# One addition and one reciprocal per head, in place of one of each for a pair of heads, in a fused attention and mixture-of-experts kernel

## The chip, the cores and the metric

The kernel runs on one core of a Trainium2 chip. The metric is the device time of one execution in microseconds (us). The core has five engines that matter here: TensorE (PE, matrix products; its weight loads are shown as PEld), VectorE (DVE), ScalarE (ACT), GpSimd (POOL), and SyncE (SP, which issues most of the DMAs). Each engine works through its own list of instructions in order; an instruction that needs the result of another engine waits for a semaphore, and everything behind it on its engine waits too.

## The reference, cut to what matters

Three layers follow one another: attention with a forget gate (4 batches, 8 heads, 576 positions, head size 64), a feed-forward layer (512 to 2048 to 512), and a mixture of experts where each token goes to its best one of 8 experts. The change touches the softmax of the attention alone:

```
scores = scale * q @ k.T + decay, with -1e9 above the diagonal
scores = scores - max(scores, axis=-1)
attn = exp(scores)
attn = attn / (sum(attn, axis=-1) + 1e-09)
out = attn @ v
```

## The kernel before, in words

The attention works on pairs of heads: 16 pairs `i` (four batches of four pairs). Each pair is cut into five units `c`, taken in the order 4, 3, 2, 1, 0. Units 0 to 3 are 128 rows of queries for each of the two heads, with 128 x (c + 1) columns of keys; unit 4 takes the last 64 rows of both heads in one tile of 128 x 576 and counts as one "head" (called `None`). So a pair has four units of two heads and one unit of one.

For each unit, `unit` (line 532 and around) lets PE compute the scores into one of two buffers in PSUM (tiles `SR`, `SRx`). Then `head` runs once for each head, as a chain of steps:

- DVE adds the decay and the mask, writes the scores into a tile `P`, and reduces each row's extreme into column `n` of a small tile `st` (128 x 8; line 582);
- ACT takes the exponential in place and adds up each row into column `2 + n` of `st` (line 587; the trace shows it as an ACTIVATE and a short read of the accumulator);
- DVE adds 1e-9 to the sums (line 592) and takes the reciprocal (line 594);
- POOL multiplies `P` by the reciprocal (line 598);
- PE transposes `P` in blocks of 128 (line 612), and DVE (head 0 of the two widest units, line 630) or ACT (the others, line 632) copies the result out of PSUM.

In the kernel before, lines 592 and 594 are issued once per unit, by head 0, for the columns of both heads together, after both heads' exponentials (event `summed`); head 1 waits for event `scaled`. Unit 4 has one column.

When all units of a pair are transposed, `weighted` multiplies by the values (lines 652 and 705) and stores the pair's output `xT` as tile `xs` to memory. A pair of heads needs eight of the `P` tiles at most (there are eight, so four units of two heads can be under way), and there are two PSUM buffers for transposes.

The order of all instructions is fixed while the program is built, by a small planner. Every step is a coroutine that asks for an engine with a planned duration and a priority (`Use("DVE", 150, fn, 0)`): the planner simulates the engines, always issues the waiting request of the lowest priority number, and adds a latency before the next step (130 ns after DVE, 150 ns after ACT, 135 ns after POOL, 200 ns after PE). Priorities: 0 for the addition, the reciprocal, the multiplication on POOL, the transposes and their copies; 0.8 for the scores and for the conversion of weights; 1 for lines 582 and 587; 1.5 for the transposes of q and k (line 442); 6 to 7 for the feed-forward layers. Planned times shape the order alone; on the chip each instruction starts when its engine is free and its semaphores are there.

Beside the attention run two other things. First, the weights of the first half of the feed-forward layer are converted in 16 pieces (tiles `wax`, `wa`): ACT (line 823), four operations on DVE (824 to 830), ACT (834), POOL (835). One piece at a time goes through, since there is one buffer `wx`. Second, the feed-forward layer's first half (tiles `hp`, `accp`, lines 880 and 1009; its elementwise steps are lines 892 to 902) takes blocks of 256 tokens. Block 0 (`px0`) is built straight from the first four pairs; a block needs all 16 pieces of weights, and there is one buffer for a block's input until the attention is over. Until the first batch is done, PE is filled with products whose result is thrown away (`warm`, line 729), at the lowest priority.

Of the kernel before, what the change touches and what calls it, by code (L numbers as in the profile page):

```python
# [14 lines left out]
ALU = mybir.AluOpType  # L15
# [60 lines left out]
class Order:  # L76
# [90 lines left out]
    def done(self, ev):  # L167
        ev.n -= 1
        if ev.n == 0:
            for g in ev.waiters:  # L170
                self.at(self.now, lambda g=g: self.step(g, None))
            ev.waiters = []

    def give(self, res, ids):
        res.ids += ids
        while res.waiters:
            gen, n = res.waiters[0]
            got = res.take(n)
            if got is None:
                return  # L180
            res.waiters.pop(0)
            self.at(self.now, lambda gen=gen, got=got: self.step(gen, got))
# [8 lines left out]
def dve(n, fn, prio=5.0, fast=False):  # L191
    return Use("DVE", 144 + n * (0.6 if fast else 1.05), fn, prio)


def act(n, fn, prio=5.0, more=0.0):
    return Use("ACT", 155 + n / 1.2 + more, fn, prio)


def pool1(n, fn, prio=5.0):
    return Use("POOL", 400 + 0.7 * n, fn, prio)  # L200
# [16 lines left out]
def mm(n, k=1):  # L217
    return k * max(111.0, n * 0.458)
# [5 lines left out]
def kernel(  # L224
# [14 lines left out]
    nc = tc.nc  # L239
# [22 lines left out]
    go, give, done = o.spawn, o.give, o.done  # L262
# [250 lines left out]
    def unit(i, c, started):  # L513

        yield qk_ok[i]
        heads = (None,) if c == 4 else (0, 1)
        gp_ = yield (p_b, len(heads))
        sl = yield (sr_b, ((0, 1), (2, 3)))
        bank = SR[sl[0] // 2]
        done(started)  # L520
        (qt, kt), z, _ = qkt[i]
        w = P * (c + 1) if c < 4 else S

        def scores():
            if c == 4:
                for n in range(2):
                    nc.tensor.matmul(bank[:, n, :S // 2], z, kt[:, S // 2 * n:S // 2 * (n + 1)],
                                     start=True, stop=i >= NSUM)
                return
            for j in range(2):  # L530
                p = slice(64 * j, 64 * j + 64)
                nc.tensor.matmul(bank[:, j, :w], qt[p, P * c:P * c + P], kt[p, :w],  # L532
                                 start=True, stop=i >= NSUM)

        def sums():
            n3 = 3 * NH
            if i == 0:
                for n in range(2):
                    if c == 4:
                        nc.tensor.matmul(bank[:, n, :S // 2], pick,  # L540
                                         cum[:NH, S // 2 * n:S // 2 * (n + 1)], start=False, stop=True)
                    else:
                        p = slice(64 * n, 64 * n + NH)
                        nc.tensor.matmul(bank[:, n, :w], ident[p, 65 * n:65 * n + 1].to_broadcast(
                            [NH, P]), cum[p, :w], start=False, stop=True)
                return
            if c == 4:
                for n in range(2):
                    nc.tensor.matmul(bank[:, n, :S // 2], picks[:n3, P * i:P * i + P],
                                     parts[:n3, S // 2 * n:S // 2 * (n + 1)], start=False, stop=True)  # L550
                return
            for j in range(2):
                h = 64 * (2 * i + j)
                nc.tensor.matmul(bank[:, j, :w], picks[:n3, h:h + 1].to_broadcast([n3, P]),
                                 parts[:n3, :w], start=False, stop=True)
        yield Use("PE", max(440, 1.72 * w), scores, 0.8, full=0.8)
        done(s_done[i])
        if i < NSUM:
            yield parts_there if i else sums_there
            yield Use("PE", mm(w if c < 4 else S // 2, 2) if i else 1.72 * w, sums, 0.8)  # L560
        yield cm_ok[i, c]
        st = ap.tile([P, 8], F32, tag="st", name=f"st{i}_{c}", bufs=10)
        summed, scaled = Event(len(heads)), Event()
        left = Event(len(heads))
        for n, j in enumerate(heads):
            p = ap.tile([P, S], F32, tag="P", name=f"P{i}_{j}{c}", bufs=NP_)
            go(head(i, j, c, p, [gp_[n]], bank, st, summed, scaled, left))
        yield left
        give(sr_b, sl)

    def head(i, j, c, p, gp_, bank, st, summed, scaled, left):
        w = P * (c + 1) if c < 4 else S
        n = j or 0
        k = 2 if c < 4 else 1
        pw = p[:, :w]
        cm, c4, _ = cms[i]
        if c < 4:
            so, pv_ = bank[:, j, :w], pw
            m = cm[:, j, :w] if i >= NSUM else cm[:, 0, 512 - w:]
        else:  # L580
            so, m, pv_ = bank[:, :, :S // 2], c4, p.rearrange("p (a b) -> p a b", a=2)
        yield dve(w + 80, lambda: nc.vector.tensor_tensor_reduce(  # L582
            out=pv_, in0=so, in1=m, scale=-0.125, scalar=3e38,
            op0=ALU.add, op1=ALU.min, accum_out=st[:, n:n + 1]), 1)
        done(left)
        done(read_ok[i, c])
        yield act(w, lambda: nc.scalar.activation(pw, pw, AF.Exp, bias=st[:, n:n + 1], scale=-1.0,  # L587
                                                  accum_out=st[:, 2 + n:3 + n]), 1, 330)
        done(summed)
        if n == 0:  # L590
            yield summed
            yield Use("DVE", 150, lambda: nc.vector.tensor_scalar(
                st[:, 4:4 + k], st[:, 2:2 + k], 1e-9, None, ALU.add), 0)
            yield Use("DVE", 150, lambda: nc.vector.reciprocal(st[:, 6:6 + k], st[:, 4:4 + k]), 0)  # L594
            done(scaled)
        else:
            yield scaled
        yield pool1(w, lambda: nc.gpsimd.tensor_scalar(pw, pw, st[:, 6 + n:7 + n], 1.0, ALU.mult,  # L598
                                                       ALU.mult), 0)
        yield pt_ok[i, j]  # L600
        dst = pt4[i][0] if c == 4 else pt[i, j][0]
        for part in ((0, 1, 2, 3), (4,)) if c == 4 else (tuple(range(c + 1)),):
            gt = yield (t_b, 1)
            T = psa.tile([P, 512], F32, tag=f"T{gt[0]}", name=f"T{i}_{j}{c}{part[0]}", bufs=1)
            last = part == (4,)

            def turn():
                for n, kb in enumerate(part):
                    if last:
                        nc.tensor.transpose(T[:64, :P], p[:, 512:S], ident)  # L610
                    else:
                        nc.tensor.transpose(T[:, P * n:P * n + P], p[:, P * kb:P * kb + P], ident)  # L612
            yield Use("PE", mm(P, len(part)), turn, 0)
            if last or c < 4:
                give(p_b, gp_)
            if c == 4:
                n = P * len(part)
                src, dh = (T[:64, :P], dst[:64, 512:]) if last else (T, dst[:, :512])
            else:
                n = w  # L620
                src = T[:, :w].rearrange("p (k q) -> p k q", q=P)
                if c < 2:
                    dh = dst[:, P * c:P * c + 384 * (c + 1)].rearrange(
                        "p (k q) -> p k q", q=384)[:, :, :P]
                else:
                    a0 = P * (c - 2)
                    dh = dst[:, a0:a0 + 384 * (c + 1)].rearrange(
                        "p (k q) -> p k q", q=384)[:, :, 256:]
            if j == 0 and c >= 2:
                yield dve(n, lambda: nc.vector.tensor_copy(dh, src), 0)  # L630
            else:
                yield act(n, lambda: nc.scalar.copy(dh, src), 0)  # L632
            give(t_b, gt)
        done(last_ok[i] if c == 4 else heads_ok[i])
# [100 lines left out]
    def attention():  # L735
        go(forget_rows())
        go(prep())
        yield Use("POOL", 3000, setup, 0)
        go(keep_warm(xs_ok[0]))
        yield sums_there  # L740
        go(loadv(0))
        for i in range(NP):
            if i + 1 < NP:
                go(loadv(i + 1))
            if i == NPAIR:
                go(hand_over())
            go(decays(i))
            go(take_pt(i))
            go(free_qk(i))
            go(weighted(i))  # L750
            for c in SEQ:
                ev = Event()
                go(unit(i, c, ev))
                yield ev
# [888 lines left out]
```

## Time and profile before

| | |
|---|---|
| median of 3 runs | 872.46 us (870.70 to 873.15) |
| profiled execution | 871.59 us, span of its instructions 870.0 us |
| busy: PE / PEld / DVE / ACT / POOL | 842.5 / 692.7 / 463.2 / 363.6 / 301.6 us |
| mean granted TensorE clock | 0.993 of 2.4 GHz |
| attention's last addition (line 592) | starts at 303.8 us |

The busy time of PE is partly modelled, since matrix products are pipelined: a PE that is busy for a whole stretch had no gap, but need not be at its peak. Gaps are named by what ended them. The profile's times are us from the start of the span.

### The profile page before, as it was taken

What the parts mean: (1) busy time and instruction counts of PE and PEld (TensorE: products, weight loads), DVE (VectorE), ACT (ScalarE), POOL (GpSimd) and SP (SyncE); (2) the same over time, 40 slices, a digit from 0 to 9 for tenths busy, and PEclk for the clock granted to TensorE, in tenths of its full rate; (3) what the DMA queues carried; (4) which work ended last, traced back from release to release, by engine and by line L of the source; (5) the groups of instructions that cost most, each with busy time, mean ns of one, the idle gap of its engine ahead of it and who ended that gap; (6) DMA issues with size and microseconds to landing.
All of it is one profiled execution on the core that took longest, in us unless ns stands there. A gap on an engine that the chain in (4) does not pass through costs nothing. (4 is left out here: it accounts for less than half of the span.)

```text
span 870.0 us, 15066 instructions
## 1 busy us (share of the span) xinstructions
PE 842.5 (97%) x5384; PEld 692.7 (80%) x5384; DVE 463.2 (53%) x1104; ACT 363.6 (42%) x842; POOL 301.6 (35%) x405
## 2 busy tenths in 40 slices
PE   9999997999999999999899999999999999999994
PEld 6765775887787799999888888888998888886683
DVE  7797977766545537767843354377643512112120
ACT  5677666565656635444533242323333112112010
POOL 2566876555544533444342122222210033000000
PEclk9999999999999999999999999999999999999998
DMA  7997666474324154323601135744431111721210
GB/s 144 179 188 178 157 165 155 119 144 118 92 80 132 46 137 97 108 93 100 225 34 49 73 122 156 213 154 142 146 112 49 48 49 49 288 75 64 82 49 25
DMA packets 153659, 100.90 MB, mean 116 GB/s; under 512 B 102724, under 2 KB 125764, under 8 KB 153584
## 3 DMA queue, kind: packets, MB, share of 16 engines
q1 hardware_dynamic: 150608, 95.43, 40.1%
q0 software_dynamic: 2784, 4.21, 1.8%
q8 instruction: 43, 0.70, 0.4%
q10 hardware_dynamic: 192, 0.30, 0.1%
q14 instruction: 32, 0.26, 0.1%
HBM read 76.33 MB, written 23.84 MB: 115 GB/s over the span
## 5 line engine op out<-in xcount | busy, mean ns | idle before, releaser
L902 POOL TENSOR_TENSOR glr<-gr,ghr 128x512 fp32r<-128x512 f32 x36 | 46.9, 1304 | 146.9 <-PE accBr L1009 87.1
L598 POOL TENSOR_SCALAR P<-P,st 128x512 f32<-128x512 f32 (+3 forms) x128 | 76.6, 611 | 39.2 <-DVE st L594 25.6
L880 PE MATMUL hr<-rx,wb 128*128 128x512 f32 (+1 forms) x384 | 88.7, 365 | 0.0
L880 PE MATMUL hm<-mx,wm 128*128 128x512 f32 (+1 forms) x336 | 87.4, 381 | 0.0
L1009 PE MATMUL accp<-ghp,wa 128*128 128x256 f32 x576 | 83.4, 287 | 2.1 <-DVE x_7b L1038 1.7
L587 ACT ACTIVATE P<-P,st 128x512 f32<-128x512 f32 (+3 forms) x128 | 71.4, 559 | 33.5 <-DVE st L582 32.4
L911 DVE SCALAR_TENSOR_TENSOR glm<-hm,ghm 128x512 fp32r<-128x512 f32 x36 | 24.8, 689 | 103.4 <-PE accBm L1017 68.7
L1009 PEld LDWEIGHTS accp<-ghp,wa 128*128 128x128 f32 x576 | 73.6, 191 | 5.4 <-issue 2.2
L910 ACT ACTIVATE ghm<-hm 128x512 fp32r<-128x512 f32 x36 | 21.5, 598 | 132.9 <-PE accBm L1017 111.6
L880 PEld LDWEIGHTS hr<-rx,wb 128*128 128x128 f32 x384 | 65.9, 189 | 12.2
L880 PEld LDWEIGHTS hm<-mx,wm 128*128 128x128 f32 x336 | 61.0, 188 | 15.6 <-issue 3.4
L902 POOL TENSOR_TENSOR glp<-gp,ghp 128x512 fp32r<-128x512 f32 x36 | 48.7, 1353 | 60.8 <-ACT ghp L901 54.3
L582 DVE CUSTOM_DVE_ANT_0 P<-SR,cm 128x512 f32<-128x512 f32 (+3 forms) x96 | 45.2, 485 | 24.9 <-PE SR L532 21.7
L612 PE MATMUL T<-ident,P 128*128 128x128 f32 x320 | 52.4, 278 | 3.4 <-POOL P L598 2.9
L632 ACT COPY pt<-T 128x512 f32<-128x512 f32 (+2 forms) x96 | 35.2, 391 | 36.5 <-PE T L612 35.7
L892 ACT ACTIVATE tr<-hr,quarter 128x512 f32<-128x512 f32 x36 | 24.7, 687 | 61.1 <-DVE gr L897 42.4
L532 PE MATMUL SR<-kt,qt 64*128 64x384 f32 (+3 forms) x224 | 45.7, 485 | 4.2 <-DVE st L582 4.1
L1017 PE MATMUL accm<-wm,ghm 128*128 128x512 f32 x160 | 49.0, 395 | 0.0
L612 PEld LDWEIGHTS T<-ident,P 128*128 128x128 f32 x320 | 36.8, 141 | 14.5 <-POOL P L598 6.3
L896 DVE SCALAR_TENSOR_TENSOR gr<-tr 128x512 f32<-128x512 f32 x36 | 25.9, 719 | 41.4 <-POOL glr L902 39.8
L1009 PE MATMUL accr<-ghr,wb 128*128 128x512 f32 (+1 forms) x160 | 47.1, 376 | 0.0
L1009 PE MATMUL accp<-glp,wa 128*128 128x256 f32 x288 | 46.3, 283 | 0.4 <-POOL glp L902 0.4
(348 smaller groups left out, 1858.9 us busy)
## 6 DMA issues: line engine op xcount, KB each, us to landing
cm<-rows SPq DMA_DIRECT2D x24, 256.0 KB, 4.7
rawq<-in_q_dram SPq DMA_DIRECT2D x64, 72.0 KB, 3.6
rawk<-in_k_dram SPq DMA_DIRECT2D x64, 72.0 KB, 3.0
xs<-xT SPq DMA_DIRECT2D x16, 288.0 KB, 2.1
x2n<-nat SPq DMA_DIRECT2D x18, 256.0 KB, 3.1
war<-in_moe_w_in_dram SPq DMA_DIRECT2D x8, 512.0 KB, 4.6
war<-in_moe_w_out_dram SPq DMA_DIRECT2D x8, 512.0 KB, 4.2
rawv<-in_v_dram SPq DMA_DIRECT2D x32, 128.0 KB, 2.7
```

Source lines behind the costliest of these rows:

```text
L532: nc.tensor.matmul(bank[:, j, :w], qt[p, P * c:P * c + P], kt[p, :w], start=True, stop=i >= NSUM)
L582: yield dve(w + 80, lambda: nc.vector.tensor_tensor_reduce(out=pv_, in0=so, in1=m, scale=-0.125, scalar=3e38, op0=ALU.add, op1=ALU.min, ac ...
L587: yield act(w, lambda: nc.scalar.activation(pw, pw, AF.Exp, bias=st[:, n:n + 1], scale=-1.0, accum_out=st[:, 2 + n:3 + n]), 1, 330)
L598: yield pool1(w, lambda: nc.gpsimd.tensor_scalar(pw, pw, st[:, 6 + n:7 + n], 1.0, ALU.mult, ALU.mult), 0)
L612: nc.tensor.transpose(T[:, P * n:P * n + P], p[:, P * kb:P * kb + P], ident)
L632: yield act(n, lambda: nc.scalar.copy(dh, src), 0)
L880: nc.tensor.matmul(oo, a[:, c, cs], x[c], start=(ip == 0 and c == 0), stop=(ip == 2 and c == KC - 1))
L896: yield dve(n, lambda: nc.vector.scalar_tensor_tensor(g, t, 0.5, t, ALU.min, ALU.mult), 2)
L902: yield pool2(n, lambda: nc.gpsimd.tensor_tensor(gl, g, f32(gh), ALU.subtract), 1)
L911: yield dve(n, lambda: nc.vector.scalar_tensor_tensor(gl, oo, 0.0, f32(gh), ALU.max, ALU.subtract), 2)
L1009: nc.tensor.matmul(acc[d][:, :w], b[:, fc, P * d:P * d + P], g, start=(fc == 0 and ip == 0 and (not narrow or d % 2 == 0)), stop=(fc == NF ...
L1017: nc.tensor.matmul(acc[a], g[:, P * a:P * a + P], b[:, fc], start=(fc == 0 and ip == 0), stop=(fc == NF - 1 and ip == 2))
```

## The change

Each head does its own addition and its own reciprocal, on its own column of `st`, as soon as its own exponential is there. The events `summed` and `scaled` go. The planned durations are 80 and 100 ns for the one-column operations, where 150 and 150 ns stood for two. Unit 4 is issued as before, with the new planned durations. The priority stays 0.

```
-            go(head(i, j, c, p, [gp_[n]], bank, st, summed, scaled, left))
+            go(head(i, j, c, p, [gp_[n]], bank, st, left))
...
-        done(summed)
-        if n == 0:
-            yield summed
-            yield Use("DVE", 150, lambda: nc.vector.tensor_scalar(
-                st[:, 4:4 + k], st[:, 2:2 + k], 1e-9, None, ALU.add), 0)
-            yield Use("DVE", 150, lambda: nc.vector.reciprocal(st[:, 6:6 + k], st[:, 4:4 + k]), 0)
-            done(scaled)
-        else:
-            yield scaled
+        yield Use("DVE", 80, lambda: nc.vector.tensor_scalar(
+            st[:, 4 + n:5 + n], st[:, 2 + n:3 + n], 1e-9, None, ALU.add), 0)
+        yield Use("DVE", 100, lambda: nc.vector.reciprocal(st[:, 6 + n:7 + n], st[:, 4 + n:5 + n]), 0)
```

## Rows read from the trace of the kernel before

**Rows 1.** The page, section 1: busy us, share of the span, instructions.
```profile
PE 842.5 (97%) x5384; PEld 692.7 (80%) x5384; DVE 463.2 (53%) x1104; ACT 363.6 (42%) x842; POOL 301.6 (35%) x405
```
**Rows 2.** Stretches: from:to, length, busy PE, PEld, DVE, ACT, POOL (instructions), clock, DMA share, GB/s.
```profile
15.00:86.00 71.00, 67.29 (x489) 45.49 (x489) 58.35 (x184) 51.17 (x140) 42.74 (x65) 0.98 0.89 175
86.00:150.00 64.00, 58.15 (x469) 45.17 (x468) 52.53 (x145) 42.76 (x112) 47.77 (x69) 1.00 0.67 159
150.00:310.00 160.00, 159.88 (x1282) 127.09 (x1282) 92.23 (x301) 96.14 (x261) 83.92 (x150) 1.00 0.42 103
...
130.00:140.00 10.00, 5.55 (x33) 3.77 (x33) 8.74 (x22) 6.37 (x18) 7.42 (x12) 1.00 0.80 157
```
**Rows 3.** The same view for the filler tile `warm` alone: PE and PEld busy.
```profile
15.00:86.00 71.00, 18.18 (x114) 15.62 (x114) 0.98 0.89 175
```
**Rows 4.** Waits of PE from 15 to 150 us: total us, times, longest.
```profile
PE SR L532 <- DVE st L582: 4.1, 4, 2.7
PE T L612 <- POOL P L598: 2.9, 6, 0.8
```
**Rows 5.** Timeline: start, us, engine, line, operation; the 15th weight piece and its user.
```profile
132.54 1.28 POOL L835 TENSOR_TENSOR wa<-wax,wa 128x512 fp32r<-128x512 f32 x1 [0.47 <-ACT wa L834]
...
134.76 0.64 PE L880 MATMUL hp<-px0h,wa 128*128 128x256 f32 x4
```
**Rows 6.** Groups of DVE instructions, whole span: count, busy us, mean ns, idle before.
```profile
L592 DVE TENSOR_SCALAR st<-st 128x2 f32<-128x2 f32 x64 | 19.4, 303 | 13.0 <-ACT P L587 13.0
...
L594 DVE RECIPROCAL st<-st 128x2 f32<-128x2 f32 x64 | 10.1, 157 | 0.7
...
L594 DVE RECIPROCAL st<-st 128x1 f32<-128x1 f32 x16 | 2.6, 160 | 0.2
```
**Rows 7.** The same groups from 15 to 150 us.
```profile
L592 DVE TENSOR_SCALAR st<-st 128x2 f32<-128x2 f32 x30 | 10.0, 334 | 4.2 <-ACT P L587 4.2
...
L594 DVE RECIPROCAL st<-st 128x2 f32<-128x2 f32 x30 | 4.6, 154 | 0.2
...
L592 DVE TENSOR_SCALAR st<-st 128x1 f32<-128x1 f32 x8 | 1.2, 146 | 1.9 <-ACT P_None L587 1.9
```
**Rows 8.** Timeline of one two-head unit at 141 us, from DVE, ACT and POOL.
```profile
141.22 0.15 DVE L592 TENSOR_SCALAR st<-st 128x1 f32<-128x1 f32 x1
141.29 0.68 DVE L582 CUSTOM_DVE_ANT_0 P<-SR,cm 128x512 f32<-128x512 f32 x1
141.34 0.72 ACT L587 ACTIVATE P<-P,st 128x512 f32<-128x512 f32 x1 [0.91 <-DVE st L582]
...
142.06 0.70 ACT L587 ACTIVATE P<-P,st 128x512 f32<-128x512 f32 x1
...
142.90 0.32 DVE L592 TENSOR_SCALAR st<-st 128x2 f32<-128x2 f32 x1 [0.84 <-ACT P L587]
...
143.60 0.69 POOL L598 TENSOR_SCALAR P<-P,st 128x512 f32<-128x512 f32 x1 [0.42 <-DVE st L594]
```
**Rows 9.** Timeline: additions of two columns and of one beside a POOL operation.
```profile
90.96 1.28 POOL L835 TENSOR_TENSOR wa<-wax,wa 128x512 fp32r<-128x512 f32 x1
91.07 1.19 DVE L592 TENSOR_SCALAR st<-st 128x2 f32<-128x2 f32 x1
...
100.58 1.27 POOL L835 TENSOR_TENSOR wa<-wax,wa 128x512 fp32r<-128x512 f32 x1 [1.56 <-ACT wa L834]
100.72 0.14 DVE L592 TENSOR_SCALAR st<-st 128x1 f32<-128x1 f32 x1
```
**Rows 10.** Timeline at the hole near 135 us: POOL, DVE, PE.
```profile
133.78 1.97 POOL L598 TENSOR_SCALAR P<-P,st 128x256 f32<-128x256 f32 x4
...
137.75 0.76 DVE L582 CUSTOM_DVE_ANT_0 P_None<-SR,cl 128x576 f32<-128x576 f32 x1 [0.74 <-POOL cl L482]
...
138.57 1.13 PE L532 MATMUL SR<-kt,qt 64*128 64x512 f32 x4 [2.73 <-DVE st L582]
```
**Rows 11.** Waits of DVE from 15 to 150 us: total us, times, longest.
```profile
DVE st L592 <- ACT P L587: 4.2, 5, 1.4
```

More of the change, by code (lines that the diff above doesn't have):

```diff
@@ L562, in unit @@
         st = ap.tile([P, 8], F32, tag="st", name=f"st{i}_{c}", bufs=10)
-        summed, scaled = Event(len(heads)), Event()
         left = Event(len(heads))
@@ L566, in unit, with head @@
             p = ap.tile([P, S], F32, tag="P", name=f"P{i}_{j}{c}", bufs=NP_)
-            go(head(i, j, c, p, [gp_[n]], bank, st, summed, scaled, left))
+            go(head(i, j, c, p, [gp_[n]], bank, st, left))
         yield left
         give(sr_b, sl)
-    def head(i, j, c, p, gp_, bank, st, summed, scaled, left):
+    def head(i, j, c, p, gp_, bank, st, left):
         w = P * (c + 1) if c < 4 else S
         n = j or 0
-        k = 2 if c < 4 else 1
         pw = p[:, :w]
```

## The prediction

> **What bounds the kernel now.** I read the page's first section, then busy time by stretches, then the waits inside the stretches that are not full. PE is busy for 842.5 of 870.0 us [rows 1], so the time is PE's work plus what PE wastes, and the change takes no work from PE. What it can alter is the waste: gaps, and filler products whose result nobody reads.
>
> The stretches say where waste can lie [rows 2]. From 150 to 310 us, the larger part of the attention, PE is busy for 159.88 of 160 us: feed-forward blocks fill whatever the attention leaves, so 34 of the 64 two-head units run under full cover. From 15 to 86 us PE is busy for 67.29 of 71 us, but 18.18 of these are filler [rows 3]: here the attention's own chain sets the pace, and DVE, busy for 58.35 us (82%), is its fullest engine. From 86 to 150 us PE idles for 64 - 58.15 = 5.85 us, 4.45 of them between 130 and 140. There the conversion of weights gates block 0: its 15th piece leaves POOL at 132.54 + 1.28 = 133.82 us, and the block's last products follow at 134.76 [rows 5]. The next block can only be loaded then. So the stretch that counts ends at about 150 us: it holds 30 units of two heads, and PE waits there for line 582 of DVE (4.1 us) and for POOL's multiplication (2.9 us) [rows 4].
>
> **The change part by part.** *Two adds for one.* In the stretch that counts, 30 two-column additions of 334 ns, 10.0 us, become 60 of one column. Eight of these stand in the same stretch at 146 ns [rows 7], so 60 x 0.146 = 8.8 us: 1.2 less. The two-column mean is high because some of these wait inside the instruction: one that starts at 91.07 us, under a POOL operation of 1.28 us, takes 1.19 us and both end within 0.02 us of each other; a one-column addition that starts at 100.72, 0.14 us into such a POOL operation, takes 0.14 us [rows 9]. So I expect the one-column form not to wait for POOL.
>
> The Trainium skill, "SBUF — State Buffer", section "Who interferes with whom", lists `tensor_scalar` among the operations that can take the port pair shared with GpSimd, the second to start being blocked for the whole instruction, and names no exception for a single column. If one column were blocked as two are, the additions would cost 60 x 0.334 = 20.0 us, 10.0 more, and the time would be about 882. The rows side with the rule for two columns and against it for one, so I give this outcome 0.02.
>
> *Two reciprocals for one.* 30 of 154 ns, 4.6 us [rows 7], become 60 at 160 ns, the one-column mean [rows 6], 9.6 us: 5.0 more. Added up, DVE's busy time in the stretch grows by 5.0 - 1.2 = 3.8 us; over all 64 units the additions go from 19.4 to 128 x 0.146 = 18.7 and the reciprocals from 10.1 to 20.5 us [rows 6], 9.7 more. But busy time overlaps: the addition at 141.22 takes 0.15 us and the next DVE instruction starts 0.07 us after it did [rows 8], so 0.08 us of it lie beside the next. With 60 more instructions, 60 x 0.08 = 4.8 us can vanish, and the net is between 3.8 - 4.8 = -1.0 and +3.8 us. I take 0: the lower end is the nearest measured overlap for every added instruction, and I keep 1 us back for those that meet a wait. After 150 us, any extra is hidden by the feed-forward products on PE.
>
> *The wait on the other head's exponential goes.* In the unit at 141 us the two exponentials start 0.72 us apart; the two-column addition starts at 142.90, after the second, and POOL's first multiplication at 143.60 [rows 8]. With its own addition head 0 can go 0.7 us sooner (0.4 for the narrowest unit, by the difference of lengths), and POOL then multiplies for head 0 while ACT is at head 1, so the unit's last multiplication is earlier as well, by about one multiplication or 0.5 to 0.7 us. What is late next is DVE itself, at 82%, so the pace of units hardly changes; the gain shows where a pair ends. The first batch's end, which lets block 0 start, comes about 0.5 us sooner: -0.5.
>
> That head 0 really need not wait for head 1 shows in the same rows: head 0's exponential writes its column of `st` from 141.34 while head 1's reduction on DVE, 141.29 to 141.97, still writes another. Columns of the tile are tracked apart.
>
> *The hole near 135 us.* There four multiplications stand in a row on POOL, 1.97 us, the mask of the next pair's tile comes behind them, DVE waits for that mask, and PE waits 2.73 us for DVE [rows 10]. Spread over two shorter stints, POOL would let the mask in earlier; I take -0.5 of the 4.45 us, an estimate between 0 and all of it, since the order is laid out anew.
>
> *The planner.* Planned DVE time per unit goes from 300 to 360 ns, and the steps that follow are planned sooner for head 0. Every instruction behind the first unit may so change its place, on all engines. That has no row; its bounds are what is wasted in the stretch that counts: downwards the 5.85 us of gaps, upwards what the rivals below give.
>
> Sum on the profiled execution: 871.6 + 0 - 0.5 - 0.5 = 870.6 us (span 870.0 and 1.6 around it, less 1.0). That execution lies 0.87 below the median of 872.46, so the forecast is 871.5.
>
> **The rivals.**
>
> *Faster: the hole closes.* If the new order lets the mask past the multiplications, the 4.45 us between 130 and 140 go, and the time is 872.5 - 4.5 = 868.0. For it: the one wait of 2.73 us and the chain behind it [rows 10], which passes through the very multiplications that move. Against it: block 0's last products sit behind the 15th weight piece at 133.82 us [rows 5], which the change does not touch.
>
> *Slower: DVE stands in line for head 0.* Each addition waits on DVE for ACT, and DVE takes nothing behind it meanwhile: the next head's line 582, the copies of transposes, the weight conversion, and through them PE's scores and ACT's exponentials. Now 5 of 30 do so in the stretch that counts, 4.2 us [rows 11]. With 60 additions in the place of 30, and the first of each two issued before the second exponential is done, another 4.2 us come on an engine that has little to spare: 872.5 + 4.2 = 876.7. It decides once DVE's idle time before line 592 exceeds about 7 us in the stretch. Against it: 25 of 30 never waited, because the planner reckons the exponential longer (912 ns for 512 columns, by its formula) than the 0.72 us that it takes.
>
> *Slower: every instruction costs its full length.* If the overlap of 0.08 us is not to be had, the 3.8 us stand: 872.5 + 3.8 = 876.3. The Trainium skill, "VectorE: DVE Perf Modes", section "Rules for kernel authors", says of chained operations that their number is to be kept small, as the flush of the pipeline comes with each; by that the change is a loss. The row at 141.22 [rows 8] speaks against the full length.
>
> *The change does not do what it says.* If the addition for head 0 still waited for both exponentials through the shared tile, nothing would come sooner, and the time stays at about 872.5. The overlap at 141.34 [rows 8] speaks against it.
>
> **How the numbers follow.** A measurement of this kernel tells no change from a change of less than about 0.3%, 2.6 us, so "same" is 869.8 to 875.1. The forecast has 0.45. The closed hole has 0.30: the sign of the head start is for it. Standing in line has 0.14, full length 0.06, one column blocked 0.02, no effect 0.03. So faster 0.30, same 0.45 + 0.03 = 0.48, slower 0.14 + 0.06 + 0.02 = 0.22. The range reaches down past the closed hole to the whole of the gaps, 872.5 - 5.85 = 866.6, and up to the line of waits, 876.7: 866.5 to 877, with about one in ten left out at either end. The forecast's own range is 870 to 874.
>
> **What would show it.** Right: 128 one-column additions near 0.15 us with none over 0.3; reciprocals 128 at 0.16; DVE's busy time up by 8 to 11 us; POOL's first multiplication of a unit starting before the second exponential has ended; block 0's first products before 88 us; PE full from 150 to 310 us. Wrong: additions of a microsecond (blocked); PE's gaps from 86 to 150 us well above or below 5.85 us (then the order decided, one way or the other); or DVE's wait before line 592 doubled. The forecast fails altogether if PE has gaps after 150 us that the kernel before does not have.

## The result, and the profile after

The changed kernel took 878.55 us (median of 6 runs, 876.87 to 879.88), the kernel before 872.37 us beside it: a ratio of 1.0075, with a 95% interval of 1.0061 to 1.0089. It is slower, by about 6 us; I had forecast no change (871.5), and the time lies above my range of 866.5 to 877. The profiled execution took 879.88 us with a span of 878.0, 8.0 us more than the span of the kernel before, so its rows show the loss somewhat larger than the medians do.

The page of the changed kernel, section 1, answers [rows 1]. PE does the same products (20 fewer of them filler) and is counted busy for 4 us more; DVE is busy for 463.5 us with 128 more instructions.

```profile
PE 846.7 (96%) x5364; PEld 693.3 (79%) x5364; DVE 463.5 (53%) x1232; ACT 362.8 (41%) x842; POOL 301.5 (34%) x405
```

The stretches of [rows 2] in the changed kernel (length; busy PE, PEld, DVE, ACT, POOL; granted clock; DMA share; GB/s):

```profile
15.00:86.00 71.00, 67.40 (x518) 48.21 (x517) 58.54 (x217) 50.80 (x140) 43.25 (x67) 1.00 0.86 169
86.00:150.00 64.00, 56.17 (x390) 38.69 (x387) 50.50 (x166) 41.50 (x108) 42.92 (x65) 0.95 0.67 161
150.00:310.00 160.00, 160.00 (x1285) 126.55 (x1285) 94.53 (x367) 93.17 (x252) 83.09 (x149) 1.00 0.43 105
...
130.00:140.00 10.00, 7.75 (x62) 5.28 (x62) 8.40 (x34) 6.33 (x21) 7.30 (x14) 1.00 0.76 150
```

The hole between 130 and 140 us shrank from 4.45 to 2.25 us, as a rival had it, but the stretch from 86 to 150 lost more elsewhere: PE idles for 7.83 us in place of 5.85, and its granted clock is 0.95 over the stretch, where it was 1.00. The same view in steps of 2 us shows how the clock goes with the gaps:

```profile
94.00:96.00 2.00, 0.93 (x5) 0.24 (x3) 1.97 (x7) 1.48 (x3) 1.94 (x4) 1.00 0.88 253
96.00:98.00 2.00, 0.52 (x2) 0.28 (x2) 1.45 (x3) 0.78 (x3) 1.90 (x4) 1.00 0.93 143
98.00:100.00 2.00, 1.83 (x12) 1.70 (x12) 0.84 (x2) 0.96 (x3) 1.87 (x4) 0.79 0.95 127
100.00:102.00 2.00, 1.88 (x7) 0.77 (x6) 2.00 (x3) 1.29 (x3) 1.55 (x2) 0.50 0.81 245
102.00:104.00 2.00, 2.00 (x10) 0.59 (x10) 1.93 (x6) 0.76 (x2) 1.45 (x2) 0.86 0.00 1
```

PE is busy for 1.45 of the 4 us from 94 to 98; then, with work again, it runs at the lower of its two levels (0.50, that is 1.2 of 2.4 GHz) for some us. The transposes wait for POOL there, which the waits of PE from 15 to 150 us sum up (total us, times, longest), against 2.9 us of [rows 4]:

```profile
PE T L604 <- POOL P L590: 7.3, 12, 1.3
...
PE SR L532 <- DVE st L580: 0.6, 1, 0.6
```

A second loss stands outside the stretch that I had counted. First the kernel before, then the changed one, from 320 to 450 us, where the first feed-forward half ends and the second begins:

```profile
320.00:450.00 130.00, 125.65 (x956) 120.39 (x955) 92.87 (x129) 58.18 (x97) 54.09 (x41) 1.00 0.41 123
```

```profile
320.00:450.00 130.00, 123.25 (x954) 118.35 (x951) 90.46 (x129) 58.69 (x96) 58.41 (x48) 0.99 0.46 133
```

To add the losses up I take, from stretches of 2 us, three things that PE spends on nothing: idle time, busy time x (1 - granted clock), and, from the view for the filler alone, the filler's busy time.

```
us lost               before                    changed
                idle  clock  filler       idle  clock  filler
  0 to  86      5.79   1.70   27.04       5.13   0.00   24.89
 86 to 160      5.87   0.00    0.35       7.82   3.30    0.00
160 to 320      0.12   0.00    0.00       0.00   0.00    0.00
320 to 450      4.35   0.00    0.00       6.77   1.67    0.00
sum                   45.2                      49.6
```

From 86 to 160 us 4.9 us more are lost, from 320 to 450 4.1, and 4.5 fewer up to 86: 4.4 in all, of the 8.0 by which the spans differ. The filler's column is too large, though, since a filler product overlaps the products beside it: PE without the filler is busy for 822.0 us before and 826.8 us after, out of 842.5 and 846.7, so that the filler alone took 20.4 and 19.9 us. Counted so, the losses differ by 6.3 us. The other 1.7 lie inside what is counted as busy, which is modelled; I could not place them. In these two executions, then, the time went to PE's gaps and to its clock after them, at two places. Whether the additional instructions or their new order made the gaps, the two profiles alone do not say.

### The profile page after: what moved, and what is told of

Its sections match the earlier page's. It is cut to its first block, busy times and chain, and to the rows that moved or that the text cites. A ratio compares the mean times of both kernels' runs of the same rounds, so it can differ in the third digit from the quotient of the medians.

```text
span 878.0 us, 15165 instructions
## 1 busy us (share of the span) xinstructions
PE 846.7 (96%) x5364; PEld 693.3 (79%) x5364; DVE 463.5 (53%) x1232; ACT 362.8 (41%) x842; POOL 301.5 (34%) x405
## 5 line engine op out<-in xcount | busy, mean ns | idle before, releaser
L872 PE MATMUL hr<-rx,wb 128*128 128x512 f32 (+1 forms) x384 | 90.9, 371 | 2.2 <-ACT rx L857 2.2
L590 POOL TENSOR_SCALAR P<-P,st 128x512 f32<-128x512 f32 (+3 forms) x128 | 75.3, 593 | 48.0 <-DVE st L589 19.9
L894 POOL TENSOR_TENSOR glp<-gp,ghp 128x512 fp32r<-128x512 f32 x36 | 50.7, 1409 | 46.4 <-ACT ghp L893 42.7
L604 PE MATMUL T<-ident,P 128*128 128x128 f32 x320 | 54.6, 279 | 8.5 <-POOL P L590 7.3
```

Source lines behind the costliest of these rows:

```text
L872: nc.tensor.matmul(oo, a[:, c, cs], x[c], start=(ip == 0 and c == 0), stop=(ip == 2 and c == KC - 1))
L894: yield pool2(n, lambda: nc.gpsimd.tensor_tensor(gl, g, f32(gh), ALU.subtract), 1)
```

## The experiments

Theory "order": the change costs by the new order that the planner lays out, whatever the operations. Theory "cost": 128 more DVE instructions cost the time. Ratios are to runs of the kernel before on the same chip in the same session (17 to 23 runs, median 870.5 in each of the three sessions), with 95% intervals.

**1. The operations alone.** Two one-column operations stand where one of two columns stood, in the same place; PE, ACT, POOL and SP keep their instructions in the same order, all of them.

```
-            yield Use("DVE", 150, lambda: nc.vector.tensor_scalar(
-                st[:, 4:4 + k], st[:, 2:2 + k], 1e-9, None, ALU.add), 0)
+            yield Use("DVE", 150, lambda: [nc.vector.tensor_scalar(
+                st[:, 4 + m:5 + m], st[:, 2 + m:3 + m], 1e-9, None, ALU.add) for m in range(k)], 0)
-            yield Use("DVE", 150, lambda: nc.vector.reciprocal(st[:, 6:6 + k], st[:, 4:4 + k]), 0)
+            yield Use("DVE", 150, lambda: [nc.vector.reciprocal(
+                st[:, 6 + m:7 + m], st[:, 4 + m:5 + m]) for m in range(k)], 0)
```

> Kernel before, with nothing altered but the operations themselves: in the place of each two-column addition stand two one-column additions back to back, and so for the reciprocals. The order on PE, ACT, POOL and SP is the same, instruction for instruction. Theory 'order' (the new order of the instructions costs the time): 872.4 as before, within 1.5 us, DVE busy about 463 + 8 us less what is saved on blocked additions. Theory 'cost' (128 more DVE instructions cost the time): near 878.

Measured: 868.96 us, ratio 0.9986 (0.9976 to 0.9996). The operations cost nothing; they save about 1.2 us (0.3 to 2.1 by the interval). The page's first section and the two groups on DVE (count, busy us, mean ns) of this kernel:

```profile
PE 843.5 (97%) x5384; PEld 694.2 (80%) x5384; DVE 461.6 (53%) x1232; ACT 363.2 (42%) x842; POOL 301.1 (35%) x405
```

```profile
L594 DVE RECIPROCAL st<-st 128x1 f32<-128x1 f32 x144 | 17.0, 151 | 0.2
L592 DVE TENSOR_SCALAR st<-st 128x1 f32<-128x1 f32 x144 | 16.6, 143 | 23.9 <-ACT P_None L587 13.2 <-ACT P L587 10.6
```

DVE is busy for 461.6 us, 1.6 less than before, with 128 more instructions. 144 reciprocals of 151 ns would be 21.7 us laid end to end; the busy time is 17.0, because neighbours overlap. That is still 4.3 us more than the 12.7 of the 80 reciprocals before; the additions make up for it, with 16.6 us in place of 21.8, since none of them is held up beside POOL any more. "Cost" falls.

**2. Own operations without the early start.** The changed kernel, with two lines added after the exponential, so that both heads wait for both sums:

```
+        done(summed)
+        yield summed
         yield Use("DVE", 80, lambda: nc.vector.tensor_scalar(
```

> The changed kernel, but each head goes on to its own addition and reciprocal only when the exponentials of both heads are there, so that the early start of head 0 is gone and the planner lays out the order anew. Theory 'order, by the early start': back to 871 to 874. Theory 'order, by any shuffle': anywhere in 868 to 880, with no relation to 872.4. Theory 'cost': near 878.

Measured: 875.89 us, ratio 1.0063 (1.0047 to 1.0079), not to be told from the changed kernel's 1.0075. No head starts early here, and the loss is there all the same: it does not need the early start, and taking that away does not bring the old order back.

**3. Planned times alone, 80 and 100.** The kernel before, its own two-column operations, and two numbers that only the planner reads:

```
-            yield Use("DVE", 150, lambda: nc.vector.tensor_scalar(
+            yield Use("DVE", 80, lambda: nc.vector.tensor_scalar(
...
-            yield Use("DVE", 150, lambda: nc.vector.reciprocal(st[:, 6:6 + k], st[:, 4:4 + k]), 0)
+            yield Use("DVE", 100, lambda: nc.vector.reciprocal(st[:, 6:6 + k], st[:, 4:4 + k]), 0)
```

> Kernel before with its two-column operations, only planned at 80 and 100 ns instead of 150 and 150: the operations are the same, the order differs in several hundred places. Theory 'order': moves by a few us in either sense (868 to 878). Theory 'cost': 872.4 within 1 us.

Measured: 882.80 us, ratio 1.0134 (1.0119 to 1.0148). With not one operation changed, this is slower than the changed kernel. Its stretch from 320 to 440 us shows most of it, 12.7 us of gaps where the kernel before has 4.35:

```profile
320.00:440.00 120.00, 107.30 (x857) 105.65 (x856) 88.18 (x122) 53.39 (x87) 59.30 (x42) 0.97 0.41 123
```

**4. The changed kernel planned at 150 and 150.** Its operations and waits stay as they are:

```
-        yield Use("DVE", 80, lambda: nc.vector.tensor_scalar(
+        yield Use("DVE", 150, lambda: nc.vector.tensor_scalar(
...
-        yield Use("DVE", 100, lambda: nc.vector.reciprocal(st[:, 6 + n:7 + n], st[:, 4 + n:5 + n]), 0)
+        yield Use("DVE", 150, lambda: nc.vector.reciprocal(st[:, 6 + n:7 + n], st[:, 4 + n:5 + n]), 0)
```

> The changed kernel, planned at 150 and 150 ns for each one-column operation: the same operations as the changed kernel in another order. Theory 'order': moves by a few us from 878.5 in either sense (872 to 882). Theory 'cost': 878.5 within 1 us.

Measured: 876.86 us, ratio 1.0073 (1.0060 to 1.0086), the same as the changed kernel's, which by this one number would have spoken for "cost". The profile does not: the second block's first products came at 134.2 us (changed kernel 149.1, kernel before 145.2), and the time won was lost again from 320 to 450 us, with 10.2 us of gaps. Two orders can end alike by different ways.

**5 and 6. The start of the second half.** In the changed kernel SyncE issues the loads of `rx`, the second half's input, 9 us later than before, behind a load of weights for which it waits until 420.50 us. First the kernel before, then the changed one (start, us, queue, line):

```profile
411.31 0.34 SPq L814 DMA_DIRECT2D wbr<-in_moe_w_out_dram  x1
411.70 1.86 SPq L861 DMA_DIRECT2D rx<-xs  x4
```

```profile
420.50 0.37 SPq L806 DMA_DIRECT2D wbr<-in_moe_w_in_dram  x1
420.91 1.93 SPq L853 DMA_DIRECT2D rx<-xs  x4
...
432.76 0.62 PE L872 MATMUL hr<-rx,wb 128*128 128x512 f32 x2
435.08 0.49 PE L872 MATMUL hr<-rx,wb 128*128 128x512 f32 x1 [1.69 <-ACT rx L857]
436.12 9.49 PE L872 MATMUL hr<-rx,wb 128*128 128x512 f32 x33 [0.54 <-ACT rx L857]
```

PE waits for `rx` twice and then takes 9.49 us for 33 products; at full speed 48 of them took 11.05 us, so 33 take 7.6. The granted clock of that stretch, in the changed kernel:

```profile
430.00:440.00 10.00, 7.31 (x33) 5.39 (x32) 9.09 (x16) 5.98 (x12) 1.96 (x2) 0.85 0.51 160
```

Both experiments let the planner load the first block of `rx` as soon as the buffers are free:

```
-        yield half0.first_done
         yield late_ok
+        go(half1.loads((0,)))
+        yield half0.first_done
         go(gates())
-        go(half1.loads())
+        go(half1.loads(range(1, NW)))
```

> The changed kernel; the planner may load the first input block of the second feed-forward half (tile rx) as soon as the attention's buffers are free, in place of after the first half's last products. Up to about 400 us the order is that of the changed kernel. Theory 'two places' (of the 6 us lost, 2 to 4 are lost where the second half starts, on rx and the clock that falls with it): 874.5 to 876.5, no wait of PE on rx, and PE's idle time from 320 to 450 us under 5.5 us. Theory 'front' (all is lost before 160 us): 878.5 within 1 us.

> Kernel before with the same earlier load of rx. PE did not wait for rx there, so both theories expect 870 to 872.5 on the scale of 871.5 to 872.4 for the kernel before; a gain of 2 us or more would mean that the early load helps whatever the order, and that the comparison with the changed kernel says little.

Measured with the changed kernel: 875.42 us, ratio 1.0048 (1.0032 to 1.0065); with the kernel before: 870.23 us, 0.9993 (0.9980 to 1.0006). About 2.4 us of the loss go with this cause in the changed kernel, and nothing in the kernel before. The interval still touches that of the changed kernel, so the size is rough. Idle time from 320 to 450 us came out at 5.99, above the 5.5 that I had named: PE no longer waits for `rx`, but meets other short waits.

```profile
86.00:160.00 74.00, 64.90 (x487) 47.61 (x487) 59.14 (x199) 48.19 (x128) 50.40 (x79) 1.00 0.62 152
320.00:450.00 130.00, 124.01 (x957) 119.50 (x956) 94.81 (x130) 59.36 (x97) 59.26 (x49) 1.00 0.43 131
```

These rows hold a warning: up to about 365 us the order is that of the changed kernel, with even more gaps from 86 to 160, and yet the clock stayed at 1.00. The old order shows the reverse. It stands unchanged, up to there, in experiments 1 and 6 (in this order below), and the clock fell in both:

```profile
86.00:160.00 74.00, 70.04 (x531) 54.70 (x529) 58.17 (x192) 48.64 (x129) 51.86 (x79) 0.98 0.63 152
86.00:160.00 74.00, 69.04 (x517) 54.04 (x519) 56.64 (x159) 47.22 (x126) 51.83 (x78) 0.95 0.61 145
```

So from 86 to 160 us the gaps tell the two orders apart (5.9, 4.0 and 5.0 us in three executions of the old one, 7.8 and 9.1 in two of the new one), and the clock of a single execution does not (0, 1.5 and 3.0 us lost, against 3.3 and 0). The clock is to be taken as a mean over runs: span x (1 - mean granted clock) is 7.5 us in the six runs of the changed kernel, 5.3, 6.1 and 5.4 in the 17, 22 and 23 runs of the kernel before beside the experiments, and 5.8 in the six of experiment 5. By that, the clock has 1.4 to 2.2 of the 6 us.

**7, 11 and 12. Planned times alone, 155, 140 and 160.** The kernel before; the two numbers 150 and 150 become 155 and 155 (shown), 140 and 140, 160 and 160.

```
-            yield Use("DVE", 150, lambda: nc.vector.tensor_scalar(
+            yield Use("DVE", 155, lambda: nc.vector.tensor_scalar(
...
-            yield Use("DVE", 150, lambda: nc.vector.reciprocal(st[:, 6:6 + k], st[:, 4:4 + k]), 0)
+            yield Use("DVE", 155, lambda: nc.vector.reciprocal(st[:, 6:6 + k], st[:, 4:4 + k]), 0)
```

> Kernel before, its two-column operations planned at 155 ns each in the place of 150: nothing else. Theory 'order is fragile' (any small change of a planned time shuffles hundreds of instructions, and the kernel before happens to have a good order): 2 to 12 us slower, with PE's idle time and lost clock grown in the stretches from 86 to 160 and 320 to 450 us. Theory 'the early start of head 0 is what hurts': within 1.5 us of the kernel before.

> Kernel before, its two-column operations planned at 140 ns each. Theory 'order is fragile': several us off the kernel before, most likely slower (873 to 882), since the four shuffled orders so far were 5 to 12 us slower. If shorter planned times were what hurts (80 and 100 gave 12 us): slower by about 2. If longer ones (155 gave 8): not slower.

> Kernel before, its two-column operations planned at 160 ns each. Theory 'order is fragile': several us off, 873 to 882, not the same as at 155. If there were a rule in the planned time, it would lie near or above the 8.4 us that 155 lost.

Measured: 155 gives 878.97 us, ratio 1.0085 (1.0068 to 1.0101); 140 gives 880.07, 1.0114 (1.0097 to 1.0131); 160 gives 879.85, 1.0103 (1.0079 to 1.0127). A planned time altered by 5 ns, with the same operations, costs as much as the whole change did. No rule in the planned time shows: shorter and longer ones lose alike. At 155 the loss stands from 320 to 450 us, by gaps (7.5 us, 4.35 before) and clock; from 86 to 160 us, where I had expected it too, the gaps are no larger than before (5.5 us against 5.9):

```profile
86.00:160.00 74.00, 68.52 (x533) 53.59 (x532) 56.22 (x157) 47.34 (x121) 49.23 (x73) 0.98 0.63 155
...
320.00:450.00 130.00, 122.48 (x930) 117.22 (x930) 85.59 (x122) 56.09 (x93) 56.88 (x46) 0.96 0.40 126
```

**8. Filler for longer.** In the changed kernel the first batch is done sooner, and the filler stops with it:

```
-        go(keep_warm(xs_ok[0]))
+        go(keep_warm(half0.x_ok[1]))
```

> The changed kernel; the planner may use filler products on PE until the second input block is loaded (near 150 us) and not only until the first batch is done (near 80 us). Theory 'clock' (3.3 us are lost before 160 us because PE's clock falls in its gaps): granted clock 1.00 from 86 to 160 us, and 874.5 to 877. Theory 'gaps alone': the filler stands in gaps and in nobody's way, 877.5 to 879.5. If the filler delays the attention: slower than 879.5.

Measured: 874.19 us, ratio 1.0036 (1.0023 to 1.0049), clear of the changed kernel's interval: 3.4 us won by 50 more products that nobody reads.

```profile
86.00:160.00 74.00, 70.37 (x539) 53.42 (x539) 57.83 (x191) 47.52 (x127) 50.06 (x77) 1.00 0.67 154
```

PE's idle time in this stretch fell from 7.82 to 3.63 us, but for 5.4 us PE had nothing but filler (its 50 products have 8.23 us, partly beside others), so idle time and filler together rose to 9.0, and it is not the gaps that paid. Clock lost over the whole run, as a mean of its 11 runs, is 4.4 us where the changed kernel loses 7.5 in another session: 3.0 of the 3.4 us, if the sessions may be compared (the kernel before moved between 5.3 and 6.1). The filler also moves some hundreds of instructions on all engines, from 93 us on, so a share of order in the gain is not excluded.

**9. Both mends together**, in the changed kernel: the edits of experiments 5 and 8.

```
-        go(keep_warm(xs_ok[0]))
+        go(keep_warm(half0.x_ok[1]))
...
-        yield half0.first_done
         yield late_ok
+        go(half1.loads((0,)))
+        yield half0.first_done
         go(gates())
-        go(half1.loads())
+        go(half1.loads(range(1, NW)))
```

> The changed kernel with both: the earlier load of rx and the filler until the second input block. Theory 'two places' (the front, by gaps and clock, and the start of the second half are separate losses): the gains add, 2.4 and 3.4 us off the changed kernel's 1.0075 of the kernel before, so 1.0005 to 1.002, about 871.5 to 872.5 on a scale of 870.5. If both remove the same loss: 1.0035.

Measured: 871.40 us, ratio 1.0011 (1.0000 to 1.0022). The gains add: of 0.75% lost, 0.11% are left, against a kernel before that has neither mend. The stretches of this run:

```profile
86.00:160.00 74.00, 70.10 (x532) 52.53 (x531) 57.02 (x189) 47.52 (x126) 49.17 (x77) 1.00 0.67 155
...
320.00:450.00 130.00, 126.01 (x966) 121.00 (x963) 93.77 (x129) 58.99 (x96) 57.32 (x48) 1.00 0.47 129
```

**10. A version against the kernel before**: its order, the four one-column operations of experiment 1, and both mends.

```
-                st[:, 4:4 + k], st[:, 2:2 + k], 1e-9, None, ALU.add), 0)
+                st[:, 4 + m:5 + m], st[:, 2 + m:3 + m], 1e-9, None, ALU.add) for m in range(k)], 0)
...
-        go(keep_warm(xs_ok[0]))
+        go(keep_warm(half0.x_ok[1]))
...
+        go(half1.loads((0,)))
+        yield half0.first_done
```

> Kernel before, with the four one-column operations of the first experiment, the earlier load of rx and the longer filler; the early start of head 0 is left out. The filler moves several hundred instructions from 86 us on. If the filler's gain is that of a held clock, as it was with the changed kernel: 866.5 to 870 on a scale of 870.5, the fastest of all. Theory 'order is fragile': 872 to 880, since the order is shuffled once more.

Measured: 869.43 us, ratio 0.9989 (0.9976 to 1.0001), not to be told from experiment 1 alone (0.9986). PE's order differs from that of experiment 1 from about 129 us on, and this time the shuffle did no harm, or no more than the mends give back. Experiment 9, with the same mends beside the change, took 871.40 us in the same session, 2 us more.

## Why the prediction was wrong

**The two adds and two reciprocals: right.** I took 0, between -1.0 and +3.8 us on DVE; the operations alone, in an unchanged order, came to about -1.2 us. All 144 one-column additions of the changed kernel lie between 109 and 156 ns, none held up by POOL, though 52 of them began when a POOL operation had at least 0.2 us to run. Those of two columns reached 1316 ns: all 27 above 200 ns began under a POOL operation, and 26 ended 0.02 to 0.03 us after it. So what the Trainium skill, "SBUF — State Buffer", section "Who interferes with whom", says `tensor_scalar` can suffer, on conditions for its operands, is seen here with two columns and not with one. The advice of the Trainium skill, "VectorE: DVE Perf Modes", section "Rules for kernel authors", to keep the count of chained operations small is not borne out by the time: 128 more of them, and it went down in experiment 1. On DVE itself each further operation did have its price there (4.3 us for 64 more reciprocals). What I said of DVE's total, 8 to 11 us more, was wrong: 0.3 more. The two groups did grow, by 7.4 us:

```profile
L589 DVE RECIPROCAL st<-st 128x1 f32<-128x1 f32 x144 | 21.8, 155 | 1.8
L587 DVE TENSOR_SCALAR st<-st 128x1 f32<-128x1 f32 x144 | 20.1, 143 | 21.0 <-ACT P L585 14.2 <-ACT P_None L585 6.5
```

but laid end to end all of DVE's instructions grew by 7.1 us (518.3 to 525.4), and 6.9 us more than before lie beside a neighbour. I had reckoned with 0.08 us of overlap for each added instruction in the stretch that counts; for the whole span, 128 x 0.08 = 10.2 us against the 9.7 more, I left it out.

**The early start: there in a quarter of the units, and without weight.** I had each unit's first multiplication start before its second exponential has ended. By the order of the `P` tiles on ACT and POOL, 16 of the 64 two-head units do so (none in the kernel before). Block 0's first products came at 80.4 us in place of 88.3, far more than the 0.5 us that I gave it. Yet experiment 3, which has no early start, had them at 80.5: the order did it. And it did not help, since block 0 still ended by the weights, its last group of products coming at 137.38 us (135 before): PE had less filler, then gaps, then a lower clock.

```profile
L872 PE MATMUL hp<-px0h,wa x64: 277/283/495, 80.4 to 137.8; 128*128 128x256 f32 x64
```

**The hole near 135 us: half closed,** 2.2 us where I took 0.5. That the change closed it is not shown: in experiment 1, in the old order, the same 10 us have 2.03 us of gaps.

```profile
130.00:140.00 10.00, 7.97 (x37) 5.76 (x39) 9.08 (x28) 5.50 (x16) 6.75 (x11) 0.83 0.72 172
```

The gap at 91 to 98 us outweighed it. There the multiplications of a pair of heads, which had stood together, were spread as I had expected; the weights' operation on POOL (line 827, 1.27 us) stands between them, and PE's transposes behind them waited (timeline of the changed kernel):

```profile
92.55 0.48 POOL L590 TENSOR_SCALAR P<-P,st 128x256 f32<-128x256 f32 x1 [1.35 <-DVE st L580]
...
93.04 1.27 POOL L827 TENSOR_TENSOR wa<-wax,wa 128x512 fp32r<-128x512 f32 x1
93.08 0.44 PE L604 MATMUL T<-ident,P 128*128 128x128 f32 x2 [1.23 <-POOL P L590]
...
94.29 0.98 POOL L590 TENSOR_SCALAR P<-P,st 128x256 f32<-128x256 f32 x1
...
95.33 0.44 PE L604 MATMUL T<-ident,P 128*128 128x128 f32 x2 [0.84 <-POOL P L590]
```

**The planner: this is the step that failed.** I wrote that every instruction "may so change its place, on all engines. That has no row; its bounds are what is wasted in the stretch that counts: downwards the 5.85 us of gaps, upwards what the rivals below give." Upwards this was no bound. Seven other orders were laid out for these operations (the changed kernel, experiments 2 and 4, and planned times of 80 and 100, 140, 155 and 160): all seven are slower, by 5.5 to 12 us of 870. An eighth, in experiment 10, did no harm, but it came with both mends. The sum had a term for each thing that the change does, and none for the order as such; in the old order the operations save 1.2 us, in the new one the kernel loses 6.

**"After 150 us, any extra is hidden by the feed-forward products on PE": true up to 310 us only.** PE is as full from 150 to 310 us as before [rows 2], but the start of the second half lost 2.4 us in gaps and 1.7 in clock, and experiment 5 ties this in part to the place of the loads of `rx` in SyncE's list. The attention, too, ended later beside the full PE: the last pair's output is stored at 320.9 us, where it was at 312.9. That lateness does not go with the time, however: experiment 3, the slowest, stores it at 311.8 us, and experiment 10, as fast as the kernel before, at 324.8. I had looked for gaps after 150 us only as a way for the forecast to fail, and gave it no chance.

**The clock: left out.** I summed idle time and filler, but a gap can also take speed from what follows it: 3.3 and 1.7 us in the profile of the changed kernel, 1.4 to 2.2 us of the 6 as a mean over runs.

**The rivals.** None explains the time. The hole closed by half, and the time rose. DVE's waits before line 587 on a two-head exponential stayed at 4.7 us from 15 to 150 us, against 4.2 [rows 11], so it did not stand in line for head 0; full length and a blocked single column fell with experiment 1; and that nothing would change fell with the time.

```profile
DVE st L587 <- ACT P L585: 4.7, 10, 1.9
```

What stays open: why this one order is better than the seven others. That it is good is measured; what makes it good is not, beyond the two stretches, of which most of the others lose in one or both. The clock has a part: its mean loss is 6.1 to 11.5 us in the seven slow orders, 5.3 to 6.1 in the kernel before, but in experiment 4 it is 6.1, and the kernel is 6.4 us slower. Nor were the last 1.7 us placed.

## What to carry to other kernels

Where a program lays out the order by simulating planned times, any edit of a planned time or of a wait draws a new order, and its price can exceed that of the edit itself: run the operations alone in the old order, and the planned times alone with the old operations, before giving either the credit. In a forecast, give such a draw a term of its own, taken from a few harmless shuffles; here these were worth 5.5 to 12 us, against 1 us for the operations. And where an engine is full for a stretch, look at the stretch behind it as well, and count for new gaps also the lower clock behind them, as a mean over several executions.

## What the runs showed of the hardware

A one-column addition takes 109 to 156 ns in all 144 places, while POOL works or not; the two-column one takes 303 ns in the mean and up to 1316 beside POOL, and the long ones end just after POOL's operation. Small DVE instructions overlap: the next mostly starts 0.07 to 0.08 us before the one in front has ended; with that, and with no addition held up by POOL, 128 more of them left DVE's busy time 1.6 us lower in experiment 1. PE's clock can fall in one execution and not in another of the same order (0.95 and 1.00 from 86 to 160 us, in the old order as in the new). And 50 products that nobody reads made a kernel 3.4 us faster, with a mean clock loss of 4.4 us in place of 7.5.
